# Moving GpSimd's two-operand subtractions to VectorE in a planned attention and MLP kernel

## The chip, the cores and the metric

The kernel runs on one core of a Trainium2 chip. The metric is the device time of one execution in microseconds; lower is better. Five queues work beside each other: TensorE (PE, with its weight loads PEld), VectorE (DVE), ScalarE (ACT), GpSimd (POOL) and SyncE (SP), which here only issues DMAs.

## The reference

Attention with a window of 128 and 4 sink columns over batch 4, 8 heads, 768 positions, head size 64; its output, 3072 x 512, goes through two matrix products with a squared ReLU between them (hidden size 2048).

```python
scores = scale * np.matmul(q, k.transpose(0, 1, 3, 2))
keep = is_sink | in_window
scores = np.where(keep, scores, -1000000000.0)
scores = scores - np.max(scores, axis=-1, keepdims=True)
a = np.exp(scores)
a = a / (np.sum(a, axis=-1, keepdims=True) + 1e-09)
attn_out = np.matmul(a, v)
x = attn_out.transpose(0, 2, 1, 3).reshape(B * S, H * D)
h = np.maximum(x @ w_in, 0.0)
out = h * h @ w_out
```

## The kernel before

**Tiling.** The 3072 tokens are cut into 8 chunks of 384. A chunk's attention is 4 steps (one for each pair of heads), 32 steps `s` in all; its products run over 16 blocks `fc` of 128 hidden columns, 128 items in all. The matmuls of the products take numbers split in a high part and a low part (the number less its high part), three matmuls for each product. So nearly everything needs a subtraction for its low part: the 32 weight rows (`row_steps`, `low`, L342), the attention output (L793), the hidden values (L853), and from step 8 on the keys (`KS`, L464) and queries (`QS`, L475). The first 8 steps are "plain": their scores are taken from unsplit numbers (L501), and chunks 0 and 1 turn their probabilities with matmuls against `ident` (L684, sinks L616). Later chunks turn them with VectorE's transposes (L714) and a trip through DRAM (`via`, `PT`).

**A weight row.** It arrives as 64-bit words (`raw`, L306). VectorE builds the number in three integer passes (L318, L325, L332), ScalarE rounds it to the high part (L338), and VectorE or GpSimd subtracts it for the low part (L342).

**An attention step.** Scores on TensorE; VectorE adds the mask, finds the row's bound and writes to SBUF (`reduce_`, L484); ScalarE takes exp with row sums (L490); `recip` adds a small term, `eps`, to the sums (L548) and inverts them (L549), both on VectorE; the probabilities are scaled (`scale`, L556: GpSimd, in the plain steps also ScalarE, L554, and VectorE); GpSimd copies and splits the sink columns (`part_sinks`, L572, L570, into `PSK`; in the turned chunks it is called `PSK_wide`); then the turning, and the product with the values (L772, L776), and the split of its result (L788 on ScalarE, L793 on VectorE).

**A product item.** 12 matmuls (L824) into one bank; ReLU (L837) and square (L841) on ScalarE; square and subtraction on VectorE (L846, L853); one item later 9 matmuls (L869). Results leave by `evacuate` (L910 copies, L923 sends).

**What sets the order.** `Plan` is a list scheduler that runs when the program is built. Each step names its engine or several engines, a cost in us, a rank, and what it reads and writes. For a step with several engines the plan takes the one on which it ends first, with an added figure for each choice: `LOW_DVE = 0.6` is added to VectorE's cost for a low part of a weight row. Steps on VectorE that are marked "port" and all steps on GpSimd hold each other off in the plan for `SHARE`, half, of their cost. The order that results is written out and each engine then works it off strictly in turn, waiting on semaphores. A plan's times are not the chip's, only the order is used.

**Set-up.** Before the plan's part, VectorE builds the masks from the two parameters (L221 to L256); the first reduction L484 stands behind them in its queue.

Of the kernel before, what the change touches and what calls it, by code (L numbers as in the profile page):

```python
# [18 lines left out]
P = 128  # L19
# [14 lines left out]
SHARE = 0.5  # L34
HOLD = 0.15
SC_DVE = 0.3
CLAIM = (True, False)
URGE = 0.5
LOW_DVE = 0.6
# [14 lines left out]
class Plan:  # L54
# [45 lines left out]
    def order(self):  # L100
        free = dict(PE=0.0, DVE=5.5, ACT=1.5, POOL=5.0, SP=0.5)
        port, landed, mode, flow = {"DVE": 0.0, "POOL": 0.0}, [], 0, 0.0
        open_ = [n for n, s in enumerate(self.steps) if s["waits"] == 0]
        while open_:
            best = {}
            for n in open_:
# [8 lines left out]
                if e == "POOL" or "port" in kind:  # L115
                    t = max(t, port["DVE" if e == "POOL" else "POOL"])
                best.setdefault(e, []).append((t, s["rank"], n, cost, kind, picks))
            chosen = None
            for e, able in best.items():
                first = min(able)[0]  # L120
                a = min((a for a in able if a[0] <= first + 0.03), key=lambda a: a[1:3])
                urgent = [x for x in able if x[0] <= first + HOLD and x[1] < a[1] - 8]
                if urgent:
                    a = min(urgent, key=lambda a: a[1:3])
                if chosen is None or a[0] < chosen[1][0]:
                    chosen = e, a
# [14 lines left out]
            else:  # L141
                done = t + cost + self.TAIL[e]
                if e == "POOL" or "port" in kind:
                    port[e] = t + SHARE * cost
# [17 lines left out]
def sink_window_attention_moe(  # L162
# [25 lines left out]
    with ExitStack() as fast:  # L188
# [30 lines left out]
        )  # L219
        parf = sb("gl1", [P, 2, 2], F32, "parf")  # L220
# [79 lines left out]
        def row_steps(n, rank):  # L300
# [39 lines left out]
            def low(e):  # L340
# [4 lines left out]
                [("DVE", 0.62, "port", LOW_DVE), ("POOL", 1.3)], rank, low, reads=[f_cell, ("w", n)], writes=[("wl", n)]  # L345
# [31 lines left out]
        VR = [("VR", x) for x in range(4)]  # L377

# [22 lines left out]
        def attention(s, rank):  # L401
# [51 lines left out]
            if not plain:  # L453
                for h, own, oth in HALVES:
# [3 lines left out]
                        ("DVE", 0.35, "port"), r,  # L458
                        lambda h=h: nc.vector.tensor_copy(KS(h)[:, 0, 0:nk], kn()[:, h, 0:nk]),  # L459
# [3 lines left out]
                        ("POOL", 1.35 if nk == 4 else 1.25), r,  # L463
                        lambda h=h: nc.gpsimd.tensor_tensor(  # L464
# [9 lines left out]
                        ("DVE", 0.6, "port"), r,  # L474
# [731 lines left out]
```

## Time and profile before

| | |
|---|---|
| median of 3 runs | 683.7 us (683.39 to 683.94) |
| profiled execution | 682.0 us, of which its span 679.8 us |
| TensorE | 659.6 us busy, 97% of the span, granted clock 0.998 |
| VectorE | 460.5 us, 68% |
| ScalarE | 374.1 us, 55% |
| GpSimd | 211.9 us, 31% |
| DMA | 104.93 MB, mean 154 GB/s |

The profile's page names a group of instructions by its line in the kernel, the engine, the operation and the tiles that it writes and reads (`out<-in`), with the count, the busy time and the mean duration of one. Matmuls are pipelined and their ends are modelled, so TensorE's busy time is an upper bound; what can be read surely is where it stands idle and for whom. In a row of waits, `A <- B` means that A stood still until B was done. The chain of work is followed backwards from the last instruction. A window such as 10:47 is a stretch in microseconds from the span's start.

### The profile page before, as it was taken

How to read it: one execution, taken by the hardware profiler on the slowest of the kernel's cores; microseconds unless marked ns; L12 is line 12 of the kernel's file. 1: busy time of each engine (PE TensorE's matmuls, PEld its weight loads, DVE VectorE, ACT ScalarE, POOL GpSimd, SP SyncE). 2: the span in 40 equal slices, each digit the busy share in tenths (PEclk: the TensorE clock that was granted, in tenths of full speed). 3: DMA queues.
4: the chain of work that ended last, by engine and by line, in shares of the span. 5: the costliest groups of instructions: out<-in, count | busy, mean ns of one | idle time of the engine just before them, and what ended most of it. 6: DMA issues, size and time to landing. Idle time of an engine off the chain costs nothing.

```text
span 679.8 us, 11460 instructions
## 1 busy us (share of the span) xinstructions
PE 659.6 (97%) x3662; PEld 573.2 (84%) x3662; DVE 460.5 (68%) x1221; ACT 374.1 (55%) x1070; POOL 211.9 (31%) x383
## 2 busy tenths in 40 slices
PE   5999899999999999999999999999999999999996
PEld 4667788898888888988888898888889888899985
DVE  7999999878888676666667666666767754242221
ACT  5887543356454444556666666666657565542221
POOL 3646443244444333223234422323332331000000
PEclk9999999999999999999999999999999999999999
DMA  7957567016868543466556767546547754310001
GB/s 242 251 168 196 174 206 218 1 37 181 243 179 226 164 133 113 126 206 187 172 153 189 220 181 219 160 144 200 171 159 210 204 164 135 124 62 1 1 0 52
DMA packets 62549, 104.93 MB, mean 154 GB/s; under 512 B 10800, under 2 KB 39216, under 8 KB 62480
## 3 DMA queue, kind: packets, MB, share of 16 engines
q1 hardware_dynamic: 62480, 104.11, 52.0%
q8 instruction: 31, 0.51, 0.3%
q14 instruction: 38, 0.31, 0.1%
HBM read 78.72 MB, written 24.38 MB: 152 GB/s over the span
## 4 chain that ended last, share of the span: by engine, by line
PE 84%; DVE 10%; ACT 2%; DMA 2%; issue 1%; POOL 1%; SPq 0%; DVEq 0%; ACTq 0%
PE bank L869 36%; PE bank L824 35%; PE bank L772 5%; PE bank L507 5%; DVE f L332 2%; DVE f L325 2%; PE bank L776 1%; PE bank L501 1%; DMA PT<-via 1%; DVE P L484 1%; DVE f L318 1%; DVE bank L846 1%; DVE w L342 1%; DVE gl L853 1%; PE bank L684 1%
## 5 line engine op out<-in xcount | busy, mean ns | idle before, releaser
L824 PE MATMUL bank<-x,w 128*128 128x384 f32 x1536 | 301.8, 338 | 0.6 <-DVE gl L853 0.6
L824 PEld LDWEIGHTS bank<-x,w 128*128 128x128 f32 x1536 | 265.9, 188 | 8.9 <-issue 1.0
L869 PE MATMUL bank<-w,gh 128*128 128x512 f32 x768 | 242.5, 397 | 0.5 <-DVE ob L910 0.5
L869 PEld LDWEIGHTS bank<-w,gh 128*128 128x128 f32 x768 | 138.8, 188 | 23.2 <-issue 1.4
L869 PE MATMUL bank<-w,gl 128*128 128x512 f32 x384 | 152.1, 396 | 0.3 <-DVE gl L853 0.3
L464 POOL TENSOR_TENSOR KS<-kn,KS 128x396 fp32r<-128x396 f32 (+1 forms) x48 | 65.0, 1355 | 238.4 <-DVE KS L459 200.8
L837 ACT ACTIVATE r<-bank 128x384 f32<-128x384 f32 x128 | 62.5, 489 | 123.3 <-PE bank L824 122.2
L846 DVE TENSOR_TENSOR bank<-bank,r 128x384 f32<-128x384 f32 x128 | 71.9, 562 | 81.0 <-ACT r L837 80.6
L490 ACT ACTIVATE P<-P,nbs 128x260 f32<-128x260 f32 (+1 forms) x192 | 93.7, 488 | 58.5 <-DVE nbs L484 57.3
L556 POOL TENSOR_SCALAR P<-P,small 128x260 f32<-128x260 f32 (+1 forms) x169 | 84.6, 516 | 63.7 <-DVE small L549 47.4
L869 PEld LDWEIGHTS bank<-w,gl 128*128 128x128 f32 x384 | 72.1, 188 | 18.1 <-DVE gl L853 1.4
L853 DVE TENSOR_TENSOR gl<-bank,gh 128x384 fp32r<-128x384 f32 x128 | 71.2, 556 | 19.8 <-ACT gh L841 10.6
L484 DVE CUSTOM_DVE_ANT_0 P<-bank,maskA 128x260 f32<-128x260 f32 x128 | 52.7, 419 | 46.5 <-PE bank L507 46.1
L841 ACT ACTIVATE gh<-r 128x384 fp32r<-128x384 f32 x128 | 66.8, 522 | 3.5 <-PE bank L869 1.0
L714 DVE STREAM_TRANSPOSE T<-P 128x384 f32<-128x384 f32 x96 | 45.3, 495 | 25.1 <-POOL P L556 23.7
L507 PEld LDWEIGHTS bank<-KS,QS 128*128 128x128 f32 x288 | 52.3, 188 | 5.8
L507 PE MATMUL bank<-KS,QS 128*128 128x260 f32 (+1 forms) x288 | 55.1, 277 | 0.0
L342 POOL TENSOR_TENSOR w<-f,w 128x512 fp32r<-128x512 f32 x20 | 29.6, 1481 | 44.5 <-ACT w L338 38.6
L788 ACT CAST x<-bank 128x384 fp32r<-128x384 f32 x32 | 15.2, 475 | 48.0 <-PE bank L776 47.9
L772 PE MATMUL bank<-PT,vn 128*64 128x256 f32 (+1 forms) x392 | 39.5, 341 | 0.9 <-DMA PT<-via 0.9
L548 DVE TENSOR_TENSOR small<-small,eps 128x3 f32<-128x3 f32 (+1 forms) x56 | 37.1, 662 | 2.9 <-ACT P L490 2.1
L772 PEld LDWEIGHTS bank<-PT,vn 128*64 128x64 f32 x392 | 25.2, 136 | 16.2 <-issue 5.7
(100 smaller groups left out, 551.5 us busy)
## 6 DMA issues: line engine op xcount, KB each, us to landing
raw<-in_moe_w_dram SPq DMA_DIRECT2D x32, 512.0 KB, 4.2
half<-in_moe_w_dram SPq DMA_DIRECT2D x64, 256.0 KB, 3.7
via<-T SPq DMA_DIRECT2D x48, 192.0 KB, 3.1
PT<-via SPq DMA_DIRECT2D x12, 768.0 KB, 4.5
via<-T SPq DMA_DIRECT2D x48, 160.0 KB, 2.8
PT<-via SPq DMA_DIRECT2D x12, 640.0 KB, 4.9
kn<-in_k_dram SPq DMA_DIRECT2D x24, 264.0 KB, 4.2
qn<-in_q_dram SPq DMA_DIRECT2D x32, 192.0 KB, 3.0
```

Source lines behind the costliest of these rows:

```text
L464: lambda h=h: nc.gpsimd.tensor_tensor(KS(h)[:, 1, 0:nk], kn()[:, h, 0:nk], f32(KS(h)[:, 0, 0:nk]), op=ALU.subtract),
L484: nc.vector.tensor_tensor_reduce(Pt(h)[:, i, o : o + n], ps_[:, 0:n], mask[:, 0:n], -SCALE, BIG, ALU.add, ALU.min, nb)
L490: nc.scalar.activation(Pt(h)[:, i, o : o + n], Pt(h)[:, i, o : o + n], AF.Exp, bias=nb, scale=-1.0, accum_out=sm[:, h, i : i + 1],)
L507: nc.tensor.matmul(bank(key)[:, 0:n], QS(h)[:, cols], flat[:, a, c0 : c0 + n], start=(a == 0), stop=(a == 1),)
L556: {"POOL": nc.gpsimd, "DVE": nc.vector}[engine].tensor_scalar(a, a, rs[:, h, i : i + 1], 1.0, op0=ALU.mult, op1=ALU.mult)
L772: nc.tensor.matmul(xo[h * D : h * D + D, qs[0] * P : qs[0] * P + len(qs) * P], vn[:, kk, h, :], rhs(), start=(n == 0), stop=False, skip_gr ...
L824: nc.tensor.matmul(bank(key)[:, 0:TOK], wi[fc][:, i, cc * P : (cc + 1) * P], xt[:, cc, :], start=(cc == 0 and j == 0), stop=(cc == NCC - 1 ...
L837: lambda key=key, r=r: nc.scalar.activation(r(), bank(key)[:, 0:TOK], AF.Relu),
L841: ("ACT", 0.41), n - 9, lambda gh=gh, r=r: nc.scalar.activation(gh(), r(), AF.Square),
L846: lambda key=key, r=r: nc.vector.tensor_tensor(bank(key)[:, 0:TOK], bank(key)[:, 0:TOK], r(), op=ALU.mult),
L853: lambda key=key, gh=gh, gl=gl: nc.vector.tensor_tensor(gl(), bank(key)[:, 0:TOK], f32(gh()), op=ALU.subtract),
L869: nc.tensor.matmul(bank(okey), gt()[:, ts_], wo[f][:, i, :], start=(f == f0 and j == 0), stop=(f == f1 - 1 and j == 2),)
```

## The change

The change is in the plan's rules and costs, and in a few steps:

1. **Rules of the plan.** Only steps marked "port" on either side hold each other off, for their whole cost; the other GpSimd steps wait for half of a VectorE "port" step and hold nothing off. Two-operand GpSimd steps (the low parts of weight rows and of keys) are now "port" steps.
2. **Low parts.** Of a weight row: no figure is added on VectorE, 0.6 on GpSimd. Of the keys: VectorE or GpSimd, whichever ends first. The copy of the keys that comes before it: VectorE or ScalarE. As built, all 32 rows' subtractions are on VectorE (12 before) and 43 of the 48 of the keys (none before); 19 of the 48 copies of the keys are on ScalarE.
3. **The small term.** ScalarE adds `eps` (an Identity activation with a bias, 56 times) and VectorE only inverts.
4. **Masks.** 10 instructions of VectorE in place of 12 between the parameters and the first reduction; `mask1` is built first and `maskA` is copied from it.
5. **The end.** The second half of the last output block gets a room of its own, so that its copy on ScalarE does not wait for the first half's copy on VectorE.
6. Several costs are set anew (0.29 and 0.32 to 0.2 for the sink columns, 0.693 to 0.7 for a product, and such).

```diff
-LOW_DVE = 0.6
+LOW_DVE = 0.0
+LOW_POOL = 0.6
+KLOW_DVE = 0.0
+KLOW_POOL = 0.0
+KS_ACT = 0.0
...
-                if e == "POOL" or "port" in kind:
+                if "port" in kind:
                     t = max(t, port["DVE" if e == "POOL" else "POOL"])
+                elif e == "POOL":
+                    t = max(t, half)
...
-                if e == "POOL" or "port" in kind:
-                    port[e] = t + SHARE * cost
+                if "port" in kind:
+                    port[e] = t + cost
+                    if e == "DVE":
+                        half = t + SHARE * cost
...
-                [("DVE", 0.62, "port", LOW_DVE), ("POOL", 1.3)], rank, low, ...
+                [("DVE", 0.62, "port", LOW_DVE), ("POOL", 1.28, "port", LOW_POOL)], rank, low, ...
...
-                        ("DVE", 0.35, "port"), r,
-                        lambda h=h: nc.vector.tensor_copy(KS(h)[:, 0, 0:nk], kn()[:, h, 0:nk]),
+                        [("DVE", 0.35, "port", 0.0), ("ACT", 0.6 if nk == 4 else 0.5, "", KS_ACT)], r,
+                        lambda e, h=h: copy(e, KS(h)[:, 0, 0:nk], kn()[:, h, 0:nk]),
...
-                        ("POOL", 1.35 if nk == 4 else 1.25), r,
-                        lambda h=h: nc.gpsimd.tensor_tensor(
+                        [
+                            ("DVE", 0.62 if nk == 4 else 0.48, "port", KLOW_DVE),
+                            ("POOL", 1.33 if nk == 4 else 1.06, "port", KLOW_POOL),
+                        ], r,
+                        lambda e, h=h: vec[e].tensor_tensor(
...
-                nc.vector.tensor_tensor(rs[:, hs], sm[:, hs], eps..., op=ALU.add)
                 nc.vector.reciprocal(rs[:, hs], rs[:, hs])
...
+                    ("ACT", 0.2), r - URGE,
+                    lambda hs=hs: nc.scalar.activation(rs[:, hs], sm[:, hs], AF.Identity, bias=eps, scale=1.0),
...
-        nc.vector.tensor_scalar(inw, rel, win, None, op0=ALU.is_lt)
-        nc.vector.tensor_tensor(inw, inw, ge, op=ALU.mult)
-        nc.vector.tensor_tensor(either, inw[:, P : 2 * P], snk, op=ALU.max)
+        nc.vector.scalar_tensor_tensor(inw_, rel, win, ge, op0=ALU.is_lt, op1=ALU.mult)
+        nc.vector.scalar_tensor_tensor(either, col, ns, inw[:, 1], op0=ALU.is_lt, op1=ALU.max)
...
-        nc.gpsimd.tensor_copy(mask1, maskA)
+        additive(mask1_[:, :, 0:P], inw)
+        additive(mask1[:, P:BS], only)
+        nc.gpsimd.tensor_copy(maskA, mask1)
+        additive(maskA[:, P:BS], snk)
...
+            rest = lambda: sb("T", [P, DM], F32, "ob_rest")
...
-                        )(ob()[:, cols], bank(okey)[:, cols]),
-                        reads=[okey] + [cell] * (x > 0),
+                        )((rest() if x else ob())[:, cols], bank(okey)[:, cols]),
+                        reads=[okey], writes=["T" if x else cell],
```

**How the order moves, first place: GpSimd's queue at the plain steps 5 and 6, counted from 0** (in the rows `P_0_517`, `P_1_521` and then `P_0_648`, `P_1_655` are probabilities of two heads of a step, `PSK_wide` their sink columns, `w_...` a weight row's low part). Before:

```order
L556 TENSOR_SCALAR P_1_521<-P_1_521,small 128x260
L572 CAST PSK_wide<-P_0_517 128x3x2x4
L572 CAST PSK_wide<-P_1_521 128x3x2x4
L570 TENSOR_TENSOR PSK_wide<-P_0_517,PSK_wide 128x3x4
L570 TENSOR_TENSOR PSK_wide<-P_1_521,PSK_wide 128x3x4
L342 TENSOR_TENSOR w_696<-f_625,w_696 128x512
L342 TENSOR_TENSOR w_706<-f_676,w_706 128x512
L342 TENSOR_TENSOR w_735<-f_684,w_735 128x512
L556 TENSOR_SCALAR P_0_648<-P_0_648,small 128x260 x2
L556 TENSOR_SCALAR P_1_655<-P_1_655,small 128x260
```

After, the same steps and the one that follows them:

```order
L569 TENSOR_SCALAR P_1_527<-P_1_527,small 128x260 x2
L585 CAST PSK_wide<-P_0_524 128x3x2x4
L585 CAST PSK_wide<-P_1_527 128x3x2x4
L583 TENSOR_TENSOR PSK_wide<-P_0_524,PSK_wide 128x3x4
L583 TENSOR_TENSOR PSK_wide<-P_1_527,PSK_wide 128x3x4
L569 TENSOR_SCALAR P_0_630<-P_0_630,small 128x260 x2
L569 TENSOR_SCALAR P_1_645<-P_1_645,small 128x260
L585 CAST PSK_wide<-P_0_630 128x3x2x4
L585 CAST PSK_wide<-P_1_645 128x3x2x4
L583 TENSOR_TENSOR PSK_wide<-P_0_630,PSK_wide 128x3x4
L583 TENSOR_TENSOR PSK_wide<-P_1_645,PSK_wide 128x3x4
L478 TENSOR_TENSOR KS_1_797<-kn_725,KS_1_797 128x396
```

The weight rows' subtractions are gone from GpSimd's queue; the first two of the keys (`KS`) are among the five that stay.

**Second place: TensorE's queue behind the values of attention step 6** (`bank_71<-x,w` is a product, `P_0_758` and `P_0_756` the probabilities of step 7, the last plain one). Before:

```order
L776 MATMUL bank_69<-SK_130,VS 128x384
L824 MATMUL bank_71<-x_148,w_800 128x384 x2
L824 MATMUL bank_71<-x_149,w_800 128x384
L684 MATMUL bank_68<-ident,P_0_758 128x128 x4
L616 MATMUL bank_67<-ident,PSK_wide 128x128 x3
```

After:

```order
L789 MATMUL bank_67<-SK_128,VS 128x384
L837 MATMUL bank_71<-x_146,w_761 128x384 x2
L837 MATMUL bank_71<-x_147,w_761 128x384
L698 MATMUL bank_68<-ident,P_0_756 128x128 x4
L837 MATMUL bank_71<-x_146,w_761 128x384 x2
L837 MATMUL bank_71<-x_147,w_761 128x384
L837 MATMUL bank_71<-x_146,w_761 128x384 x2
L837 MATMUL bank_71<-x_147,w_761 128x384
L630 MATMUL bank_69<-ident,PSK_wide 128x128 x3
```

Six matmuls of a product now stand between the turning of the probabilities and that of the sink columns. On VectorE, for the same step, before:

```order
L332 SCALAR_TENSOR_TENSOR f_851<-raw_721,f_851 128x512
L548 TENSOR_TENSOR small<-small,eps 128x6
L549 RECIPROCAL small<-small 128x6
L846 TENSOR_TENSOR bank_70<-bank_70,r_560 128x384
L853 TENSOR_TENSOR gl_586<-bank_70,gh_579 128x384
L342 TENSOR_TENSOR w_893<-f_851,w_893 128x512
```

and after:

```order
L350 TENSOR_TENSOR w_858<-f_795,w_858 128x512
L859 TENSOR_TENSOR bank_70<-bank_70,r_560 128x384
L866 TENSOR_TENSOR gl_581<-bank_70,gh_575 128x384
L333 SCALAR_TENSOR_TENSOR f_860<-raw_754,f_860 128x512
L562 RECIPROCAL small<-small 128x6
```

The inversion now stands behind the product's two passes (L859, L866) and one integer pass, where it stood ahead of them.

**Third place: VectorE's queue in a later chunk**, around the keys of one head. Before:

```order
L459 CAST KS_1_3043<-kn_2878 128x396
L853 TENSOR_TENSOR gl_606<-bank_71,gh_597 128x384
L548 TENSOR_TENSOR small<-small,eps 128x3
L549 RECIPROCAL small<-small 128x3
L475 TENSOR_TENSOR QS_1_3036<-qn_2872,QS_1_3036 64x384
```

After:

```order
L859 TENSOR_TENSOR bank_71<-bank_71,r_583 128x384
L478 TENSOR_TENSOR KS_1_3034<-kn_2858,KS_1_3034 128x396
L866 TENSOR_TENSOR gl_607<-bank_71,gh_598 128x384
L489 TENSOR_TENSOR QS_1_3049<-qn_2872,QS_1_3049 64x384
L562 RECIPROCAL small<-small 128x3
```

The addition (L548) is gone, and the keys' subtraction stands in VectorE's queue, its copy being on ScalarE here.

More of the change, by code (lines that the diff above doesn't have):

```diff
@@ L101, in order @@
         free = dict(PE=0.0, DVE=5.5, ACT=1.5, POOL=5.0, SP=0.5)
-        port, landed, mode, flow = {"DVE": 0.0, "POOL": 0.0}, [], 0, 0.0
+        port, landed, mode, flow, half = {"DVE": 0.0, "POOL": 0.0}, [], 0, 0.0, 0.0
         open_ = [n for n, s in enumerate(self.steps) if s["waits"] == 0]
@@ L124, in order @@
                     a = min(urgent, key=lambda a: a[1:3])
-                if chosen is None or a[0] < chosen[1][0]:
+                if chosen is None or a[0] < chosen[1][0] or (e == "POOL" and a[0] <= chosen[1][0] + 0.001):
                     chosen = e, a
@@ L344, in row_steps @@
             add(
-                [("DVE", 0.62, "port", LOW_DVE), ("POOL", 1.3)], rank, low, reads=[f_cell, ("w", n)], writes=[("wl", n)]
+                [("DVE", 0.62, "port", LOW_DVE), ("POOL", 1.28, "port", LOW_POOL)], rank, low, reads=[f_cell, ("w", n)], writes=[("wl", n)]
             )
@@ L377, in sink_window_attention_moe, with copy @@
         VR = [("VR", x) for x in range(4)]
+        def copy(engine, dst, src):
+            nc.scalar.copy(dst, src) if engine == "ACT" else nc.vector.tensor_copy(dst, src)
         def sinks(b, rank):
@@ L473, in attention @@
                     add(
-                        ("DVE", 0.6, "port"), r,
+                        ("DVE", 0.585, "port"), r,
                         lambda h=h, own=own, oth=oth: nc.vector.tensor_tensor(
@@ L542, in attention @@
                     add(
-                        ("ACT", 0.5 if n > P else 0.4), r - URGE, lambda h=h, i=i, n=n, o=o: exp(h, i, n, o),
+                        ("ACT", 0.505 if n > P else 0.385), r - URGE, lambda h=h, i=i, n=n, o=o: exp(h, i, n, o),
                         reads=[("nb", s, h, i), P_cell(h)], writes=[(P_cell(h), i), sm_cell, ("e", s, h, i)],
@@ L584, in attention @@
                         _, n, _, o = block(i)
-                        pool = ("POOL", 0.46 if n > P else 0.33)
+                        pool = ("POOL", 0.47 if n > P else 0.37)
                         add(
@@ L607, in attention @@
             own_sinks = [(psk_cell, h, *x) for h in range(2) for x in ((), (1,))]
-            def copy(engine, dst, src):
-                nc.scalar.copy(dst, src) if engine == "ACT" else nc.vector.tensor_copy(dst, src)
             if turned:
@@ L694, in attention @@
                     )
-                    cost = 0.08 + off / 1024
                     add(
-                        [("ACT", cost), ("DVE", cost, "", CP_DVE)], r - URGE,
+                        [("ACT", 0.04 + off / 1190), ("DVE", 0.08 + off / 1000, "", CP_DVE)], r - URGE,
                         lambda e, buf=buf, off=off, key_t=key_t: copy(e, buf()[:, 0:off], bank(key_t)[:, 0:off]),
```

57 lines of the change are left out of this document (28 added, 29 removed).

## The prediction

> **What bounds the kernel now.** I read the page's line of engines first, then busy time by stage, who TensorE waited for, and the chain of work in two stages.
>
> ```profile
> PE 659.6 (97%) x3662; PEld 573.2 (84%) x3662; DVE 460.5 (68%) x1221; ACT 374.1 (55%) x1070; POOL 211.9 (31%) x383
> ...
> core 0: us, PE busy (x) PEld busy (x) DVE busy (x) ACT busy (x) POOL busy (x), PEclk, DMA share, GB/s
> 0.00:10.00 10.00, 4.97 (x25) 4.28 (x27) 6.46 (x40) 4.30 (x14) 3.93 (x18) 1.00 0.64 172
> 10.00:47.00 37.00, 32.87 (x220) 22.72 (x216) 36.28 (x118) 32.78 (x101) 19.52 (x40) 1.00 0.79 232
> 47.00:73.00 26.00, 25.36 (x155) 19.49 (x154) 25.76 (x63) 19.99 (x52) 16.62 (x23) 1.00 0.67 204
> 73.00:128.00 55.00, 52.16 (x271) 45.81 (x272) 52.49 (x89) 23.18 (x45) 20.31 (x18) 1.00 0.54 165
> 128.00:589.00 461.00, 460.13 (x2579) 405.90 (x2579) 312.66 (x857) 267.79 (x802) 151.53 (x287) 1.00 0.58 169
> 589.00:673.00 84.00, 84.00 (x420) 74.99 (x418) 26.39 (x58) 25.70 (x59) 0.00 (x0) 1.00 0.05 17
> ```
>
> TensorE is the bound, and from 128 us on nothing else is: it stands idle 0.87 us in 461 and not at all in the 84 after them. All that a better order can win lies in its idle time between 10 and 589 us: 4.13 + 0.64 + 2.84 + 0.87 = 8.5 us. Up to 128 us VectorE is as full as TensorE: 114.5 of 118 us busy, 3.5 idle. The next views say whom TensorE waited for, and what the chain runs over from 74 to 128 us.
>
> ```profile
> PE bank L501 <- DMA kn<-in_k_dram: 5.0, 2, 4.6
> PE bank L616 <- POOL PSK_wide L570: 3.1, 2, 2.3
> PE bank L684 <- POOL P L556: 2.4, 4, 1.2
> PE bank L772 <- DMA PT<-via: 0.9, 1, 0.9
> ...
> by line: DVE f L332 21.6%; DVE f L325 16.9%; issue 8.5%; DVE bank L846 8.1%; DVE w L342 7.6%; DVE f L318 7.0%; DVE gl L853 5.4%; PE bank L869 5.2%; ACT w L338 4.5%; PE bank L824 3.9%; DVE ob L910 2.4%; POOL PSK_wide L572 2.3%; DVE QS L475 2
> ```
>
> The first wait is the first load, which the change leaves alone. The longest wait that is left is 2.3 us for GpSimd's sink columns, and from there to 128 us the chain runs over VectorE's weight rows.
>
> **The change, part by part.** *VectorE's ledger.* What does a two-operand pass of GpSimd do to VectorE? Minimum, median and maximum of the same pass, then the means by kind:
>
> ```profile
> L332 DVE SCALAR_TENSOR_TENSOR f<-raw,f x32: 653/684/1731, 17.6 to 127.6; 128x512 int32<-128x512 int32 x32
> L325 DVE SCALAR_TENSOR_TENSOR f<-raw,f x32: 651/681/1792, 16.1 to 125.3; 128x512 int32<-128x512 int32 x32
> L318 DVE TENSOR_SCALAR f<-raw x32: 410/418/1224, 15.4 to 124.3; 128x512 int32<-128x512 int32 x32
> L548 DVE TENSOR_TENSOR small<-small,eps x56: 145/876/1307, 12.2 to 566.3; 128x3 f32<-128x3 f32 x48, 128x6 f32<-128x6 f32 x8
> L342 DVE TENSOR_TENSOR w<-f,w x12: 679/688/1353, 21.3 to 129.8; 128x512 fp32r<-128x512 f32 x12
> ...
> L332 DVE SCALAR_TENSOR_TENSOR f<-raw,f 128x512 int32<-128x512 int32 x32 | 29.4, 926 | 0.2
> L325 DVE SCALAR_TENSOR_TENSOR f<-raw,f 128x512 int32<-128x512 int32 x32 | 23.4, 742 | 0.0
> L318 DVE TENSOR_SCALAR f<-raw 128x512 int32<-128x512 int32 x32 | 14.9, 484 | 0.0
> L342 DVE TENSOR_TENSOR w<-f,w 128x512 fp32r<-128x512 f32 x12 | 8.9, 746 | 1.1 <-ACT w L338 1.0
> L342 POOL TENSOR_TENSOR w<-f,w 128x512 fp32r<-128x512 f32 x20 | 29.6, 1481 | 44.5 <-ACT w L338 38.6 <-DMA qn<-in_q_dram 5.9
> ```
>
> An addition of three numbers takes 0.15 us at best and 0.88 at the median: it is held. The weight rows' excess over their medians is 32 x (926 - 684) = 7.7, 32 x 61 = 2.0, 32 x 66 = 2.1 and 12 x 58 = 0.7: 12.5 us, all before 130 us. Which of GpSimd's passes hold it? Two stages:
>
> ```profile
> L332 DVE SCALAR_TENSOR_TENSOR f<-raw,f 128x512 int32<-128x512 int32 x7 | 5.4, 783 | 0.0
> L556 POOL TENSOR_SCALAR P<-P,small 128x260 f32<-128x260 f32 (+1 forms) x17 | 9.9, 593 | 15.9 <-DVE small L549 11.3 <-ACT x L788 4.6
> L342 POOL TENSOR_TENSOR w<-f,w 128x512 fp32r<-128x512 f32 x3 | 4.3, 1424 | 4.2 <-ACT w L338 4.2
> ...
> L332 DVE SCALAR_TENSOR_TENSOR f<-raw,f 128x512 int32<-128x512 int32 x18 | 17.0, 947 | 0.1
> L342 POOL TENSOR_TENSOR w<-f,w 128x512 fp32r<-128x512 f32 x11 | 15.9, 1447 | 33.4 <-ACT w L338 27.5 <-DMA qn<-in_q_dram 5.9
> ```
>
> From 10 to 47 us (first rows), 17 scaling passes and 3 two-operand ones go with an excess of 0.1 us a pass; from 73 to 128 us, 11 two-operand ones with 0.26. The excess follows the two-operand passes, so I take it to go with them.
>
> Up to 130 us VectorE then gains 20 weight-row subtractions, 20 x 0.69 = 13.8 us, and loses 12.5 of excess and eight additions of the plain steps at 0.15, 1.2: a sum of +0.1 us. So the plain stage, where VectorE is full, does not get shorter by this: 0, between -1 and +1 for what the order does to it.
>
> *Steps 8 to 31.* VectorE loses 48 additions and 19 copies of keys, and gains 43 subtractions:
>
> ```profile
> L548 DVE TENSOR_TENSOR small<-small,eps 128x3 f32<-128x3 f32 x48 | 35.8, 746 | 2.9 <-ACT P L490 2.1
> L459 DVE CAST KS<-kn 128x528 fp32r<-128x528 f32 (+1 forms) x46 | 18.0, 395 | 1.5 <-DMA kn<-in_k_dram 1.5
> ...
> L475 DVE TENSOR_TENSOR QS<-qn,QS x48: 552/554/827, 93.7 to 547.1; 64x384 fp32r<-64x384 f32 x48
> ```
>
> No row has a subtraction of keys on VectorE. By the nearest, it is over 0.55 (384 columns) and near 0.69 (512, above): 23.7 to 29.7 us for 43, and I take 27, since half of them have 528 columns. Off go 35.8 and 19 x 0.395 = 7.5: 16 us less in the stage. It buys next to nothing, because TensorE idles only 0.87 us there, in one wait for `PT`. What leads to that DMA loses the held addition and the keys' passes ahead of the scaling on GpSimd; bounds 0 to 0.87, I take 0.4.
>
> *ScalarE* gains 56 additions, 0.2 us each by its shortest activation below, and 19 copies, taken at 0.5 (a 128x256 copy is 0.37 below): 21 us on 374, hidden in its idle 45%. In the full stage it is 32.78 of 37 us busy, and six additions are 1.2 of the 4.2 that are left; without that cover exp would be late by as much.
>
> *Waits added.* The inversion now waits for ScalarE, in whose queue the addition follows the last exp; a subtraction of keys in VectorE's queue waits for a copy, and so for the keys' DMA, with the product's L866 behind it. Of 46 copies above all waits for that DMA are 1.5 us together, so I cost it at nothing.
>
> *The wait at 72.7 us.* TensorE's row, and GpSimd's ahead of it:
>
> ```profile
> 72.10 0.60 PE L684 MATMUL bank<-ident,P 128*128 128x128 f32 x4
> 75.02 0.55 PE L616 MATMUL bank<-ident,PSK_wide 128*128 128x128 f32 x3 [2.32 <-POOL PSK_wide L570]
> ...
> 70.11 3.29 POOL L556 TENSOR_SCALAR P<-P,small 128x260 f32<-128x260 f32 x4 [1.02 <-DVE small L549]
> ```
>
> GpSimd scales four blocks in 3.29 us; in the new order it has two of them, 1.6 us less. Six product matmuls are put ahead of the sink columns' turning: by the page's 659.6 us for 3662 matmuls, 0.18 each in the mean, they are 1.1 us of cover, and I count 1.0. Against it the inversion stands behind two product passes and an integer pass, up to 1.5 us later. 2.32 - 1.6 - 1.0 + (0 to 1.5) leaves a wait of 0 to 1.2. I take 0.6, a gain of 1.7 (1.1 to 2.3). Next late are the product's low parts.
>
> *The ends.*
>
> ```profile
> 2.04 0.20 ACT L206 ACTIVATE warm<-warm 128x1 f32<-128x1 f32 x1
> 4.39 0.16 DVE L225 SCALAR_TENSOR_TENSOR par<-parf,neg 128x2 f32<-128x2 f32 x1
> 6.64 0.29 DVE L484 CUSTOM_DVE_ANT_0 P<-bank,mask 128x128 f32<-128x128 f32 x1
> ...
> 673.10 0.42 DVE L910 COPY ob<-bank 128x256 f32<-128x256 f32 x1 [0.68 <-PE bank L869]
> 673.56 0.37 ACT L910 COPY ob<-bank 128x256 f32<-128x256 f32 x1 [0.56 <-DVE ob L910]
> ```
>
> Twelve instructions take 2.25 us up to the first reduction, 0.19 each; two fewer are 0.4, given back in part since the first inversion now stands behind 17 reductions and not 16: 0.1. The second copy starts up to 0.46 us sooner, but the first half's send is still ahead of its own: 0.1.
>
> **Sum.** 1.7 + 0.4 + 0.1 + 0.1, and 0.1 for 47 to 73 us: 2.4 us less. The profiled execution took 682.0 us (span 679.8 and 2.2 around it) and would take 679.6; it lies 1.7 under the median of 683.7, which becomes 681.3.
>
> **Rivals.** *More is won.* If VectorE also lets the plain stage go faster, TensorE's idle time of 8.5 us goes but for the first chain (2.4 for the scaling and 0.8 of 3.1 for the sink columns): 5.3 and the ends 0.2, 678.2 us. For it speaks VectorE's 36.28 of 37 us; against it the ledger's +0.1. In the Trainium skill, "Perfetto Trace Analysis", section on the most-contended engine, room on TensorE is to be judged by weight loads and not by matmul time: 84% would leave 16%. The trace bears it out in part: without any wait, from 589 us on, loads are busy 74.99 of 84 us, so 89% is full here.
>
> *Nothing is won.* From 74 to 128 us the chain is VectorE's, and there the new subtractions (11 x 0.69 = 7.6) weigh as much as the excess (18 x 0.26 = 4.7 and some 2.7 of the rest). What TensorE gains at 72.7 it then loses waiting for low parts: 683.4.
>
> *Slower.* The excess does not go with the two-operand passes, because GpSimd's scaling passes hold VectorE too. If half of it stays, VectorE has 6.3 us more up to 130 us and 3.5 idle to hide it: 2.8 later, less 0.2, 686.3. It decides once more than 3.5 of the 12.5 stay. For it: scaling passes on GpSimd beside VectorE's take 0.59 us in the mean of the first stage; against: the excess by stage. "Advanced Engine Details and Errata" of the Trainium skill, "VectorE Performance Modes", notes that GpSimd instructions, of whatever kind, and two-port VectorE instructions block each other, which is this case. The two stages above agree with it only for two-operand passes.
>
> **Numbers.** Forecast 0.48 (679.7 to 682.3), more 0.12, nothing 0.24, slower 0.16. From no change 0.2%, 1.4 us, can be told: faster 0.60, same 0.24, slower 0.16. Range 677.5 to 686.0: from the first rival's price to nearly the last one's.
>
> **What would show it.** VectorE's L340, L333 and L326 at their medians with almost no excess; no two-operand rows of weights on GpSimd; the wait of L630 under 1.2 us; VectorE near 445 us; TensorE's idle from 10 to 589 us near 6. It is wrong if weight rows on VectorE keep means over 0.8 us, if 10 to 47 us holds more than 5 us of idle TensorE, or if TensorE waits for low parts (L866) after 74 us.

## The result and the profile after

The changed kernel takes 678.5 us in the median (683.4 for the kernel before, run on the same chip): the ratio is 0.9935, with a 95% interval of 0.9920 to 0.9949, so between 3.5 and 5.5 us less. One of the five executions of the changed kernel took 2531.2 us and is left out of the ratio. The forecast was 681.3, in a range of 677.5 to 686.0. The profiled execution took 678.0 us, its span 676.2 us, 3.6 us less than the span before.

The page's line of engines, busy time by stage with the columns of the table before, and TensorE's waits:

```profile
PE 658.2 (97%) x3662; PEld 573.3 (85%) x3662; DVE 445.5 (66%) x1211; ACT 392.5 (58%) x1142; POOL 125.2 (19%) x319
...
10.00:47.00 37.00, 30.98 (x198) 21.88 (x198) 34.80 (x114) 32.26 (x107) 18.03 (x37) 0.91 0.77 240
47.00:73.00 26.00, 26.00 (x167) 20.11 (x167) 25.52 (x62) 20.55 (x56) 9.55 (x18) 1.00 0.61 185
73.00:128.00 55.00, 54.81 (x291) 48.90 (x290) 53.47 (x103) 25.90 (x49) 1.81 (x5) 1.00 0.52 169
128.00:589.00 461.00, 461.00 (x2584) 406.54 (x2583) 300.19 (x843) 285.62 (x866) 91.96 (x243) 1.00 0.58 170
...
PE bank L515 <- DMA kn<-in_k_dram: 5.4, 3, 4.6
PE bank L630 <- POOL PSK_wide L583: 3.5, 3, 3.1
PE bank L698 <- POOL P L569: 1.6, 3, 1.2
PE bank L630 <- DVE nbs L498: 0.8, 1, 0.8
```

From 47 us on TensorE stands idle for 0.19 us, where it was 0.64 + 2.84 + 0.87 before. From 10 to 47 us it is the other way: 6.0 us idle, 4.1 before, and a granted clock of 0.91. Gain and loss can be dated. The rows show when TensorE starts three things: the value matmuls of step 6, the first matmul of product item 16, that of item 32; first of before, then of after.

```profile
71.29 0.44 PE L776 MATMUL bank<-SK,VS 128*128 128x384 f32 x1
125.06 1.22 PE L824 MATMUL bank<-x,w 128*128 128x384 f32 x6
207.96 0.87 PE L824 MATMUL bank<-x,w 128*128 128x384 f32 x4
```

```profile
72.39 0.44 PE L789 MATMUL bank<-SK,VS 128*128 128x384 f32 x1
122.64 2.25 PE L837 MATMUL bank<-x,w 128*128 128x384 f32 x12
204.37 0.87 PE L837 MATMUL bank<-x,w 128*128 128x384 f32 x4
```

Step 6 starts 1.1 us later than before, item 16 2.4 earlier, item 32 3.6 earlier; after that the two kernels keep their distance to the end. So the account is +1.1 up to step 6, -3.5 from there to item 16, -1.2 to item 32.

*Where -3.5 comes from.* TensorE's queue at the sink columns of step 7:

```profile
73.56 1.29 PE L837 MATMUL bank<-x,w 128*128 128x384 f32 x6
75.03 0.55 PE L630 MATMUL bank<-ident,PSK_wide 128*128 128x128 f32 x3 [0.19 <-POOL PSK_wide L583]
```

The wait that was 2.32 us is 0.19: six product matmuls run ahead of it, and GpSimd has fewer blocks to scale. Gone too are two waits for VectorE in that stage, whose rows in before are these; behind them the stretch from step 6 to item 16, of before and of after:

```profile
PE bank L869 <- DVE ob L910: 0.5, 1, 0.5
PE bank L869 <- DVE gl L853: 0.3, 1, 0.3
...
71.30:125.10 53.80, 50.66 (x267) 44.42 (x266) 51.43 (x87) 23.31 (x45) 21.29 (x18) 1.00 0.57 177
```

```profile
72.40:122.60 50.20, 50.01 (x266) 44.55 (x265) 48.94 (x94) 24.24 (x47) 2.41 (x6) 1.00 0.57 185
```

The same matmuls, with 0.19 us of idle time and not 3.14: 2.1 + 0.5 + 0.3 = 2.9 of 3.5; the other 0.6 lies in matmuls that ran closer together. VectorE does 94 passes in 48.9 us there, 0.52 each, where it did 87 in 51.4, 0.59 each. *Where -1.2 comes from:* the wait of 0.9 for `PT` is not there any more; the other 0.3 lies in matmuls that ran closer together.

*VectorE.* The rows that held the excess:

```profile
L350 DVE TENSOR_TENSOR w<-f,w 128x512 fp32r<-128x512 f32 x32 | 22.8, 716 | 0.1
L333 DVE SCALAR_TENSOR_TENSOR f<-raw,f 128x512 int32<-128x512 int32 x32 | 22.5, 714 | 0.0
L340 DVE SCALAR_TENSOR_TENSOR f<-raw,f 128x512 int32<-128x512 int32 x32 | 21.6, 681 | 0.0
L326 DVE TENSOR_SCALAR f<-raw 128x512 int32<-128x512 int32 x32 | 12.8, 423 | 0.0
L478 DVE TENSOR_TENSOR KS<-kn,KS 128x528 fp32r<-128x528 f32 (+1 forms) x43 | 27.5, 640 | 1.1
```

L340 has a mean of 0.68 us where L332 had 0.93: against the medians of before some 2 of 12.5 us of excess are left, 32 x (0.714 - 0.681) and 32 x (0.716 - 0.688). The keys' 43 subtractions cost 27.5 us, the forecast had 27.

*What is new ahead of step 6.* The largest wait there is a stall at the first attention step; that it is the source of the +1.1 is not shown (e6 below takes it away, and step 6 comes no sooner). GpSimd's passes, VectorE's, TensorE's wait and ScalarE's queue, then two single microseconds by engine (the granted clock is the third number from the end):

```profile
14.97 2.53 POOL L585 CAST PSK_wide<-P 128x16 fp32r<-128x16 f32 x1
...
14.88 0.75 DVE L326 TENSOR_SCALAR f<-raw 128x512 int32<-128x512 int32 x2
15.56 1.27 DVE L333 SCALAR_TENSOR_TENSOR f<-raw,f 128x512 int32<-128x512 int32 x2
16.76 0.67 DVE L340 SCALAR_TENSOR_TENSOR f<-raw,f 128x512 int32<-128x512 int32 x1
19.21 0.19 DVE L562 RECIPROCAL small<-small 128x6 f32<-128x6 f32 x1 [1.77 <-ACT small L593]
...
17.83 0.69 PE L630 MATMUL bank<-ident,PSK_wide 128*128 128x128 f32 x2 [3.10 <-POOL PSK_wide L583]
...
18.61 0.36 ACT L388 CAST SK<-bank 32x256 fp32r<-32x256 f32 x1 [3.01 <-PE bank L630]
...
16.00:17.00 1.00, 0.00 (x0) 0.00 (x0) 1.00 (x3) 0.00 (x0) 1.00 (x1) 0.50 0.99 376
23.00:24.00 1.00, 1.00 (x13) 0.73 (x10) 1.00 (x3) 1.00 (x4) 1.00 (x1) 1.00 0.91 254
```

A copy of 16 columns, 0.19 us elsewhere, lies on GpSimd for 2.53 us while VectorE runs five passes over two weight rows. TensorE waits 3.1 us for it, ScalarE's copy of the turned sinks waits for TensorE, and the addition of `eps` for the next step stands behind that copy: VectorE's inversion waits 1.77 us. And from 16 us on TensorE has half its clock, until between 22 and 23 us. The Trainium skill, "TensorE: Matmul & The Clock Gate", Part 1, says that the array falls to half its clock after an idle window of about 3.4 us, and that these windows run freely. Here it fell some 1.3 us after the last matmul had ended (17.83 - 3.10 = 14.73), in a stretch that was thinly filled before that (1.7 us busy in the 3 us from 12 to 15); so less than a whole idle window was enough.

### The profile page after: what moved, and what is told of

Same layout as the page of the kernel before. It is cut to its first block, busy times and chain, and to the rows that moved or that the text cites. A ratio compares the mean times of both kernels' runs of the same rounds, so it can differ in the third digit from the quotient of the medians.

```text
span 676.2 us, 11302 instructions
## 1 busy us (share of the span) xinstructions
PE 658.2 (97%) x3662; PEld 573.3 (85%) x3662; DVE 445.5 (66%) x1211; ACT 392.5 (58%) x1142; POOL 125.2 (19%) x319
## 4 chain that ended last, share of the span: by engine, by line
PE 89%; DVE 7%; POOL 1%; issue 1%; DMA 1%; ACT 0%; SPq 0%; DVEq 0%; POOLq 0%
PE bank L882 39%; PE bank L837 38%; PE bank L785 5%; PE bank L521 5%; DVE P L498 2%; PE bank L789 1%; DVE w L350 1%; DVE f L333 1%; DVE f L340 1%; DVE f L326 1%; DVE P L569 1%; DMA kn<-in_k_dram 1%; POOL PSK_wide L585 1%; DVE gl L866 0%; PE bank L515 0%
## 5 line engine op out<-in xcount | busy, mean ns | idle before, releaser
L859 DVE TENSOR_TENSOR bank<-bank,r 128x384 f32<-128x384 f32 x128 | 72.0, 563 | 77.4 <-ACT r L850 76.8
L882 PEld LDWEIGHTS bank<-w,gl 128*128 128x128 f32 x384 | 72.1, 188 | 16.9
L866 DVE TENSOR_TENSOR gl<-bank,gh 128x384 fp32r<-128x384 f32 x128 | 71.1, 556 | 19.1 <-ACT gh L854 10.1
L504 ACT ACTIVATION_READ_ACCUMULATOR P<-P,nbs 128x1 f32 x192 | 36.0, 188 | 0.0
L498 DVE CUSTOM_DVE_ANT_0 P<-bank,mask 128x128 f32<-128x128 f32 (+1 forms) x64 | 22.0, 353 | 19.3 <-PE bank L521 19.0
L374 ACT ACTIVATE sq<-sq,theta 128x256 bf16<-128x256 bf16 x64 | 32.2, 503 | 1.1
```

The source lines that it names most:

```text
L498: nc.vector.tensor_tensor_reduce(Pt(h)[:, i, o : o + n], ps_[:, 0:n], mask[:, 0:n], -SCALE, BIG, ALU.add, ALU.min, nb)
L504: nc.scalar.activation(Pt(h)[:, i, o : o + n], Pt(h)[:, i, o : o + n], AF.Exp, bias=nb, scale=-1.0, accum_out=sm[:, h, i : i + 1],)
L859: lambda key=key, r=r: nc.vector.tensor_tensor(bank(key)[:, 0:TOK], bank(key)[:, 0:TOK], r(), op=ALU.mult),
L866: lambda key=key, gh=gh, gl=gl: nc.vector.tensor_tensor(gl(), bank(key)[:, 0:TOK], f32(gh()), op=ALU.subtract),
L882: nc.tensor.matmul(bank(okey), gt()[:, ts_], wo[f][:, i, :], start=(f == f0 and j == 0), stop=(f == f1 - 1 and j == 2),)
```

## The experiments

Ratios are to the kernel before, run on the same chip; that of the change itself is 0.9935. The last columns are starts of TensorE's work in each profile, as in the rows above.

| kernel | ratio, 95% interval | step 6 | item 16 | item 32 |
|---|---|---|---|---|
| before | 1 | 71.3 | 125.1 | 208.0 |
| after | 0.9935, 0.9920 to 0.9949 | 72.4 | 122.6 | 204.4 |
| e1 low parts back | 1.0044, 1.0028 to 1.0061 | 72.7 | 126.5 | 208.4 |
| e2 addition back | 0.9961, 0.9948 to 0.9974 | 72.5 | 123.1 | 203.6 |
| e3 first sinks on VectorE | 1.0004, 0.9992 to 1.0016 | 76.1 | 126.6 | 208.3 |
| e6 first rows whole | 0.9930, 0.9915 to 0.9945 | 72.9 | 123.2 | 204.9 |
| e7 e3 and e6 together | 0.9944, 0.9928 to 0.9960 | 73.0 | 123.8 | 205.5 |
| e8 keys back | 0.9919, 0.9901 to 0.9937 | 72.1 | 122.2 | 204.0 |
| e10 old costs | 0.9938, 0.9925 to 0.9950 | 74.1 | 124.1 | 205.9 |
| e11 one cost, 0.02 us more | 0.9903, 0.9889 to 0.9918 | 72.7 | 122.7 | 204.5 |
| e12 no third integer pass | 0.9926, 0.9912 to 0.9939 | 70.9 | 121.1 | 202.8 |

The last columns say where the gain lies. TensorE's matmuls between step 6 and item 32 are the same in all of these kernels (726 or 727 in the traces; 713 in e2, where one attention step's products with the values come later). They take 131.8 to 132.5 us in after and in every experiment that leaves the weight rows' low parts on VectorE and has these matmuls, 136.7 in before and 135.6 in e1. The rest of what sets these kernels apart up to item 32 is when step 6 comes.

**e1: the plan's rules and the low parts as before.**

```diff
-LOW_DVE = 0.0
+LOW_DVE = 0.6
...
-                [("DVE", 0.62, "port", LOW_DVE), ("POOL", 1.28, "port", LOW_POOL)], rank, low, ...
+                [("DVE", 0.62, "port", LOW_DVE), ("POOL", 1.3)], rank, low, ...
...
-                        [("DVE", ..., KLOW_DVE), ("POOL", ..., KLOW_POOL)], r,
+                        ("POOL", 1.35 if nk == 4 else 1.25), r,
```

> The plan's rules and the low parts are as before (weight rows' subtractions mostly on GpSimd, all of the keys' on GpSimd, copies of keys on VectorE); the small term on ScalarE, the masks and the last room stay as changed. Theory A, the gain is that VectorE is no longer held by two-operand GpSimd passes: the gain goes, 682.5 to 686 us, VectorE's weight rows back at means of 0.75 us or more (L340 0.71 at least), 2 us or more of idle TensorE between 73 and 128 us. Theory B, the gain is that the held additions of the small term left VectorE (35.8 us of its time): most of it stays, 678.5 to 680.5 us.

Measured 685.7 us, 1.0044: theory A's range, and slower than the kernel before. VectorE's third integer pass, and TensorE's longest waits from 73 to 131 us:

```profile
L336 DVE SCALAR_TENSOR_TENSOR f<-raw,f 128x512 int32<-128x512 int32 x32 | 30.1, 949 | 0.2
...
PE bank L875 <- DVE ob L917: 1.5, 1, 1.5
PE bank L623 <- POOL PSK_wide L576: 1.2, 1, 1.2
PE bank L875 <- DVE gl L859: 0.3, 1, 0.3
```

The held passes are back at 0.95 us, and with them TensorE's waits for VectorE, 1.8 us, and for the sink columns, 1.2. (Of its other waits for VectorE one, 1.2 us, comes after 205 us, where no weight row is left; the rest lie before 47 us.) Of the whole gain, the low parts with their rules are the part that counts; the rules were not tried apart from the low parts. Why e1 is slower than before as well is not shown.

**e2: the addition back on VectorE.**

```diff
-                    ("ACT", 0.2), r - URGE,
-                    lambda hs=hs: nc.scalar.activation(rs[:, hs], sm[:, hs], AF.Identity, bias=eps, scale=1.0),
+                    ("DVE", 0.22), r - URGE, lambda hs=hs: recip(hs),
```

> Only the addition of the small term is back on VectorE, all else as after. Theory A: nothing holds the additions now, so 48 of them take 0.15 to 0.25 us each and not 0.75, at most 10 us of VectorE's time in steps 8 to 31 where it has room; in the first 25 us VectorE no longer waits for ScalarE (1.77 us at 17.4 in the trace after), so the time is 676.5 to 679. Theory B, the additions were the gain: 681 us or more.

Measured 681.0, 0.9961: theory B's time, at its edge. The additions themselves, by the smallest, the median and the longest, and the one long wait that TensorE has after 47 us:

```profile
L562 DVE TENSOR_TENSOR small<-small,eps x56: 119/164/901, 11.7 to 565.3; 128x3 f32<-128x3 f32 x48, 128x6 f32<-128x6 f32 x8
...
216.51 1.52 PE L782 MATMUL bank<-PT,vn 128*64 128x256 f32 x16 [1.81 <-DMA via<-T]
```

The median is 0.16 us where it was 0.88: with GpSimd's two-operand passes mostly gone nothing holds the additions, as theory A had it. At item 32 this kernel stands 0.8 us ahead of after, but 13 matmuls, 1.5 us of one attention step, come only after that; then it waits 1.8 us for a transfer through DRAM, late in this order. Controls e10 and e11 show how little it takes to move such a wait, so the 1.8 us by which e2 is slower are not shown to be the price of the addition.

**e3: the first step's sink columns on VectorE; e6: three integer passes of the first four rows as one step; e7: both.**

```diff
+            sinks_at = [("DVE", 0.15)] * 2 if s == 0 else [("POOL", 0.2)] * 2
...
-                        ("POOL", 0.2), r - URGE + 0.01, lambda h=h: part_sinks(h, False),
+                        sinks_at, r - URGE + 0.01, lambda e, h=h: part_sinks(e, h, False),
```

```diff
+            if n < 4:
+                add(("DVE", 1.75, "port"), rank, whole, reads=[raw_cell], writes=[f_cell])
+            else:
...
```

> As after, but the four small passes over the first step's sink columns (L585, L583 there) are VectorE's and not GpSimd's. Theory A, the 3.1 us for which TensorE stood still at 14.7 us and the half clock from 16.0 to 22.6 us come from one GpSimd pass of 128x16 held for 2.5 us by five VectorE passes, and from 47 us on nothing gives that back: the long wait and the half clock go and the time is 1.2 to 3 us under after, 675.5 to 677.3. Rival, VectorE has no room up to 47 us and swallows it: the wait goes, but the time is within 0.7 us of after's 678.5.

Measured 683.0, 1.0004: outside both. The stall at 14.7 us was gone (TensorE's L632 came at 14.37), and a worse one came in its place, for GpSimd's three scalings of the next step:

```profile
16.41 5.47 POOL L569 TENSOR_SCALAR P<-P,small 128x128 f32<-128x128 f32 x3 [2.70 <-DVE small L562]
...
21.48 2.18 PE L700 MATMUL bank<-ident,P 128*128 128x128 f32 x9 [2.23 <-POOL P L569]
```

Two of the three last 2.4 and 2.7 us. So not that one pass, but GpSimd behind a run of VectorE's passes was the trouble, and I took the runs apart:

> As after, but the three integer passes of each of the first four weight rows are one step of the plan, so they stand behind each other and each depends on the one before it; in after two rows' passes alternate and none depends on the one before it. Theory C: GpSimd waits for one pass at most, TensorE's wait at 14.7 us falls from 3.1 to under 1.2 us, the clock stays whole, and the time is 675.5 to 678.0. Theory D: the wait stays at 2 us or more and the time is 678.3 to 680.

> The edit of e3 (the first step's sink columns on VectorE) and that of e6 (three passes of a row as one step) together. Theory C: what e3 lost (4.4 us against after) came from two GpSimd scalings of 2.4 and 2.7 us behind a row of VectorE passes; they fall under 1.3 us and the time is 675.5 to 678. Theory D: they stay long and the time is 681 or more.

e6 measured 678.9, e7 679.8. In e6 the wait for the sinks fell to 1.4 us (theory C had under 1.2) and the clock stayed whole; step 6 nevertheless came at 72.9 us, and the ratio is that of after. e7 against e3 is 0.6% faster: the long scalings are gone, and the time lies between the two theories' ranges. So the long passes went as theory C had it, and it is wrong about what that is worth: after's early stall costs nothing that the rest of the first 70 us does not take as well. That the rows taken whole are what removes them is not shown either: in e11 below, where the two rows come in turn as in after, the same copy lasts 0.38 us.

**e4, e5, e9: the port by itself.** Kernels that only run VectorE's and GpSimd's passes beside each other.

> Computes nothing of the reference (writes zeros); seven kinds of VectorE pass, six in a row (16 of the tiny addition), each alone and beside three kinds of GpSimd pass: a scaling by one number (128x260), a copy of 16 columns, a subtraction of two operands (128x512). Theory A, a two-operand GpSimd pass holds VectorE's passes that read and write SBUF by two ports or two operands, a one-operand GpSimd pass does not and is itself held: beside the subtraction VectorE's shift, join, sub, scale and tiny passes have means 0.3 us or more above those alone, psum and copy none; beside scaling and the 16 columns all are within 0.05 us of those alone, and the first 16-column copy lasts 1.5 us or more beside shift (six by 0.34) and 3 us or more beside join or sub. Theory B, GpSimd passes of whatever kind hold VectorE: means 0.2 us or more above also beside scaling.

Rows of e4, for VectorE's join (two operands in SBUF) alone and beside GpSimd's scaling and subtraction, then a pass that reads PSUM, then GpSimd's passes alone and beside the join:

```profile
L82 DVE SCALAR_TENSOR_TENSOR djoin_gnone<-d_a,d_b 128x512 int32<-128x512 int32 x6 | 4.1, 691 | 0.2
L82 DVE SCALAR_TENSOR_TENSOR djoin_gscale<-d_a,d_b 128x512 int32<-128x512 int32 x6 | 4.8, 798 | 0.2
L82 DVE SCALAR_TENSOR_TENSOR djoin_gsub<-d_a,d_b 128x512 int32<-128x512 int32 x6 | 7.0, 1162 | 0.2
L87 DVE TENSOR_TENSOR dpsum_gsub<-bank,d_b 128x512 f32<-128x512 f32 x6 | 4.1, 690 | 0.2
...
L94 POOL TENSOR_TENSOR gsub_dnone<-p_a,p_b 128x512 f32<-128x512 f32 x3 | 3.8, 1262 | 0.2
L94 POOL TENSOR_TENSOR gsub_djoin<-p_a,p_b 128x512 f32<-128x512 f32 x3 | 4.9, 1628 | 0.2
L92 POOL TENSOR_SCALAR gscale_dnone<-p_a,one 128x260 f32<-128x260 f32 x4 | 1.9, 484 | 0.3
L92 POOL TENSOR_SCALAR gscale_djoin<-p_a,one 128x260 f32<-128x260 f32 x4 | 3.3, 825 | 0.3
L93 POOL COPY gsinks_djoin<-p_a 128x16 f32<-128x16 f32 x4 | 2.7, 666 | 0.2
```

The engines take turns. Three GpSimd subtractions hold three of VectorE's six joins, for 6 x (1.162 - 0.691) / 3 = 0.94 us each of the 1.26 that one lasts; four scalings hold four joins for 6 x (0.798 - 0.691) / 4 = 0.16 each of 0.48; beside the 16 columns the joins have their 0.691. A pass that reads PSUM is not held at all (0.690 us, 0.689 alone). So theory A is right on the large price and on PSUM, and wrong in that a one-operand pass would be free, on GpSimd or on VectorE, whose plain copy takes 0.90 us beside the subtraction and 0.43 alone; B is right that a scaling holds, with less than it put. Theory A had the 16 columns wrong too: they last 0.67 us beside the join, not 3. "Advanced Engine Details and Errata" of the Trainium skill, section "VectorE Performance Modes", which has GpSimd instructions and two-port VectorE instructions block each other, is borne out for GpSimd passes of both kinds, at a sixth of the price for the short one.

> Computes nothing of the reference (writes zeros); rows of VectorE passes with or without a break between them, alone and beside GpSimd passes (three scalings of 128x260, three copies of 16 columns, two subtractions of 128x512). Theory C, GpSimd gets in only where VectorE's row of two-port or two-operand passes breaks (a pass that depends on the one before it, or one that reads PSUM): where six join passes all write one tile the first 16-column copy lasts under 1.0 us, as in the probe before (0.66), where they write six tiles it lasts 3 us or more, eight shifts hold it 2 us or more, and with a PSUM pass as each third it lasts 1.0 to 1.7 us. Theory D, they take turns pass by pass whatever the row: 0.6 to 0.8 us in all of these, and the 2.5 us in the kernel are something else.

```profile
L102 POOL TENSOR_SCALAR gscale_djoinsame<-p_a,one 128x260 f32<-128x260 f32 x3 | 2.6, 881 | 0.1
L102 POOL TENSOR_SCALAR gscale_djoinfree<-p_a,one x3: 1422/1426/1440, 28.3 to 31.1; 128x260 f32<-128x260 f32 x3
L103 POOL COPY gsinks_djoinfree<-p_a x3: 654/662/668, 32.9 to 34.1; 128x16 f32<-128x16 f32 x3
```

Where VectorE's six joins write six tiles a scaling of 0.48 us lasts 1.43, where all write one tile 0.88: it waits 0.95 us or 0.40, less than two passes of 0.69 or less than one. For the 16 columns (0.66) and the subtraction (1.70) it makes no difference. GpSimd is not shut out for the whole run, as theory C had it; theory D fits.

> Computes nothing of the reference (writes zeros). VectorE's six integer passes of two weight rows as the kernel has them, in turn (alternate: two shifts, two joins, two joins) or row by row (whole), beside two GpSimd passes of three kinds (a scaling of 128x260, the copy of the sink columns, their subtraction), first with the DMA queues empty, then beside a stream of 512 KB loads. In e5 a GpSimd pass got in after two VectorE passes at most. Theory E, the loads make the difference: alternate is 1.5 us at most when quiet and over 2 us when loaded. Theory F, the alternating kinds make it: over 2 us in alternate, quiet or loaded, and under 1.5 us in whole. Theory G, neither: 1.5 us at most in all, and the 2.5 us of the kernel stay unexplained.

```profile
L109 POOL TENSOR_SCALAR probs<-probs,one x2: 907/1110/1314, 29.6 to 30.6; 128x260 f32<-128x260 f32 x2
```

The loads here started at once and filled the queues from 5 to 40 us, and GpSimd's passes of the first phase ran before VectorE's. So eight of the twelve phases were loaded, with the rows in turn in five of them, and the rows in turn were not tried with the queues empty. The longest GpSimd pass of all was 1.31 us, a scaling, loaded, with the rows in turn. That is theory G as far as it was tried: the turns explain waits up to 1 us, and the 2.2 to 2.7 us that after, e3, e8 and e10 show once or twice before 22 us stay open.

**e8: the keys back on GpSimd and VectorE's copies, the weight rows as after.**

```diff
-                        [("DVE", 0.35, "port", 0.0), ("ACT", 0.6 if nk == 4 else 0.5, "", KS_ACT)], r,
+                        ("DVE", 0.35, "port"), r,
...
-                        [("DVE", ..., KLOW_DVE), ("POOL", ..., KLOW_POOL)], r,
+                        ("POOL", 1.35 if nk == 4 else 1.25, "port"), r,
```

> As after, but the keys' copies are all VectorE's and all 48 of the keys' subtractions GpSimd's, as before; the weight rows' subtractions stay on VectorE. Theory A1, the part for the keys wins only the 0.9 us wait for the transposed probabilities: 678.7 to 680.0, with VectorE's small passes held in steps 8 to 31 at no cost. Rival, it wins nothing: 677.8 to 678.7. Rival, held passes come back as waits of TensorE: 680.5 or more.

Measured 678.3, 0.9919: the rival "it wins nothing". With 48 two-operand passes on GpSimd in steps 8 to 31 TensorE has no wait after 47 us, none for `PT` either. So of the low parts it is those of the weight rows that count, and the wait for `PT` did not go because of the keys. Nor is there one in e1; of all these kernels only before and e2, with the addition on VectorE, wait for such a transfer.

**e10, e11: controls. No step of the kernel changes, only costs in the plan, and by them the order and, for a few passes, the engine** (VectorE runs 1214 and 1215 instructions, 1211 in after). e10 has the first edit below and the six other costs of before, e11 the last edit alone.

```diff
-                            ("PE", 0.7, 0), n + 0.5 + 0.1 * t, second,
+                            ("PE", 0.693, 0), n + 0.5 + 0.1 * t, second,
...
-                    ("ACT", 0.2), r - URGE,
+                    ("ACT", 0.22), r - URGE,
```

> As after, but the plan's costs that were set anew (sink columns, scaling on GpSimd, exp, a product, the copy of transposed probabilities, the queries' subtraction) are as before; nothing that an engine executes changes, only the order. If the order is a detail, 678.5 within 0.7 us. If the order that the list scheduler happens to find is worth as much as the parts of the change, outside 677.5 to 679.5, either way.

> As after, but the plan counts 0.22 us in place of 0.20 for the addition of the small term on ScalarE: a control, nothing that is executed changes but the order. If e2's loss of 2.4 us is the addition itself, this stays within 0.7 us of 678.5. If orders found by the list scheduler scatter by 2 us, this is as likely to be off by 1 to 3 us as e2 was.

e10 measured 679.7 us, by its ratio of 0.9938 as after; e11 677.5 us, 0.9903: 2.2 us less than after by the ratios and 1.0 by the medians themselves, from a change of 0.02 us in one cost. The order alone is worth 1 to 2 us here. e1 (7.4 us from after) and e3 (4.7) are far outside that, e2 (1.8) and e8 (1.1) are not. Two controls are few, and e3, which moves only four small passes, shows that a small edit can cost more.

**e12: VectorE relieved.**

```diff
-                lambda: nc.vector.scalar_tensor_tensor(
-                    f(), raw()[:, :, 0], 29, f(), op0=ALU.logical_shift_right, op1=ALU.bitwise_or
-                ),
```

> As after without the third integer pass of each weight row (L340, so the lowest three bits of the weights are left out): VectorE has 32 x 0.68 = 21.8 us less to do, all before 130 us. If VectorE holds TensorE up to 73 us in after (its idle time and its half clock there, 5.9 us from 10 to 73 us and some 2.6 us of half clock), the time falls by 2.5 to 6 us, 672.5 to 676. If TensorE waits there for GpSimd and the first loads and not for VectorE, it stays within 1 us, 677.5 to 679.5.

Measured 678.6, 0.9926: as after, the second case. From 90 us on VectorE has plenty of room, and one wait for it came later (from 128 us on):

```profile
90.00:128.00 38.00, 38.00 (x192) 34.36 (x191) 21.55 (x41) 13.67 (x27) 0.00 (x0) 1.00 0.23 77
...
PE bank L875 <- DVE ob L910: 0.8, 1, 0.8
```

21.8 us less work for VectorE bring item 32 forward by 1.6 us, and 0.8 of it goes again into that wait. In after VectorE is full from 10 to 128 us, but that is hardly what TensorE waits for.

## Why the prediction was right, and where its steps were off

The direction, the range and the mechanism held: VectorE's passes are no longer held, and the wait at 72.7 us goes. The size did not: 4.9 us less in the medians, 4.0 between the profiled executions (before's lay 1.7 us under its median, after's 0.6), where 2.4 was forecast. 678.5 lies outside the forecast's own band, 679.7 to 682.3, next to the price of the first rival. By its terms:

- **The wait at 72.7 us**: -1.7 forecast, -2.1 measured, for the two reasons given: GpSimd's scaling takes 1.36 us in place of 3.29, and the six matmuls give 1.0 of cover; the inversion comes 1.0 later, counted from step 6. The remaining wait of 0 to 1.2 was taken at 0.6 and is 0.19. Right.
- **The rest of that stage: the step that failed.** It was put at nothing by the ledger (+0.1 us for VectorE). The ledger held: the last weight row is subtracted at 130.5 us, at 129.8 before, and VectorE's sum is 445.5 us, 445 forecast. But a sum says when VectorE is done with all, not when it is done with what TensorE waits for. Two short waits for VectorE, 0.5 and 0.3 us, stood in the waits and had no term; they went, since a pass that TensorE needs is no longer queued behind held ones; in e1, with the held passes, both are back at 1.5 and 0.3. With the 0.6 by which the matmuls ran closer that is 1.4 us where nothing stood. e12 shows the same from the other side: an engine that is full is not for that reason late.
- **The wait for `PT`**: -0.4 forecast, -0.9 measured, the upper bound. Of the reason given, fewer passes ahead of it, the keys' part is not borne out: in e8 the keys are back and the wait is not. The additions may have a part in it, but in e2 they are unheld and a wait for such a transfer is 1.8 us; the cause stays open.
- **10 to 47 us**: put at 0, between -1 and +1; it is +1.1 at step 6, and TensorE's idle time there, 6.0 us, passed the 5 us named as a sign of failure. Two sentences of the prediction failed here. That in ScalarE's queue "the addition follows the last exp": it follows a copy that waits for TensorE, and VectorE stood for 1.77 us. And GpSimd's scaling and sink passes had been priced without VectorE's port passes in front of them, though the new order runs five of those in a row. That the sum hardly suffered was luck of the kind that e6 shows: taking that stall away is worth nothing.
- **The ends**: the first reduction starts at 6.57 us, at 6.64 before, so 0.1 as forecast. At the end nothing was won: the second copy still waits 0.56 us behind VectorE's, room or no room.

```profile
6.57 0.29 DVE L498 CUSTOM_DVE_ANT_0 P<-bank,mask 128x128 f32<-128x128 f32 x1
...
669.98 0.37 ACT L924 COPY ob_rest<-bank 128x256 f32<-128x256 f32 x1 [0.56 <-DVE ob L924]
```

- **The rivals.** "More is won" named 678.2 and was nearer than the forecast, in the number and from 47 us on in the way: it took all of TensorE's idle time there, 4.35 us, and 4.16 of it went. The 0.9 that it put before 47 us did not come; idle time there grew by 1.9, and e12, with VectorE relieved, brings step 6 forward by 1.5 us only. "Nothing is won" had TensorE waiting for low parts of the weights after 74 us; there is no such wait. "Slower" asked whether the excess stays because GpSimd's scalings hold VectorE too. They do, by 0.16 us each (e4), but that is a sixth of what a subtraction costs.

What stays open: what sets the time of step 6, which lies between 70.9 and 73.0 us in after, e1, e2, e6, e7, e8, e11 and e12 whatever VectorE has to do; and the GpSimd passes of over 2 us.

## What to carry to other kernels

Count a GpSimd pass that reads two SBUF operands at its price for VectorE as well (0.94 us held for 1.26 us of work here), and let it run only where no one waits for what stands behind it: in the steady steps it cost nothing, among the weight rows, with the rules that place them, 3 to 5 us between step 6 and item 32 (136.7 and 135.6 us against 131.8 to 132.5). Price a change by the passes that the matmul engine waits for and not by the sum of an engine's work: 21.8 us taken off a full engine moved the time by nothing. Where a list scheduler sets the order, run a control that changes only a cost; here 0.02 us in one cost moved the time by 1 to 2 us, and no smaller difference says anything about the part that was edited.

## What the runs showed of the hardware

A VectorE pass that reads and writes only the SBUF, a plain copy of 128x512 too, and a GpSimd pass exclude each other in turns. VectorE is held for three quarters of a GpSimd subtraction (0.94 of 1.26 us), a third of a scaling (0.16 of 0.48) and none of a 16-column copy (0.20); passes that read PSUM are untouched. A GpSimd scaling waits 0.40 us where VectorE's passes write one tile and 0.95 where they write six (0.88 and 1.43 us for 0.48). "SBUF — State Buffer" of the Trainium skill, in "SBUF: two separate sides", calls it an exclusive lock on a shared pair of ports, held for the whole instruction; the runs agree on the exclusion, and show it shorter than the recorded pass by about 0.3 us.

TensorE's clock fell to half within a wait of 3.1 us and came back some 5 us after it was busy again.
